# Narrowing w3 and w_out by quarters, a new order of the first loads, wider list one-hots and larger grants

## The chip, the cores and the metric

The kernel runs on one core of one Trainium2 chip. The metric is device time in microseconds: the median of 3 runs of the kernel before is 763.98 us (761.05 to 764.02). All engines of the core work at once, each in its own order: TensorE (PE; its loads of weights stand as PEld), VectorE (DVE), ScalarE (ACT), GpSimd (POOL), and SyncE (SP), which issues most transfers.

## What is computed

Three parts, each on the result of the one before:

```
attention: 4 batches, 8 heads, 576 tokens, 64 per head; heads 0-3 see the last 32 keys,
           heads 4-7 every 4th of the last 128          -> x  [2304, 512]
x2 = ((x @ w1) * (x @ w2)) @ w3 @ w_out                  w1, w2 [512, 1024], w3 [1024, 1024], w_out [1024, 512]
routing:   logits = x2 @ w_gate [512, 8]; all (token, expert) pairs in falling order of logit,
           each token taken once, each expert takes at most 288
out[t] = relu(x2[t] @ e1[e]) @ e2[e]   for the expert e of token t; e1 [8, 512, 1024], e2 [8, 1024, 512]
```

w1, w2, w3 and w_out come as 64-bit floats. The inputs are laid out for the loads beforehand; nothing else is done outside the chip.

## The kernel before

Every product runs as three products of a high and a low part (`mm(h, h)`, `mm(h, l)`, `mm(l, h)`), so each weight is split in two. A 64-bit weight is first narrowed on VectorE by three integer operations (`steps64`, lines 133, 135, 137) into a 32-bit tile `f`, of which there are two.

**Opening and batches.** Attention is a generator over 36 tiles of 64 queries (9 per batch of the input). Each `next(att)` emits half of a tile's work, software pipelined: scores of tile t (L176), its masked maximum (L190), the exponentials (L197), the normalization on GpSimd (L204), transposes of tile t-2 (L210), the product with the values for t-3 (L223), and the output split of t-4 (L243 to L246). The output of a tile stands in the single PSUM bank "rt" until L245 and L246 have read it. The queries of tile t+3 (`qk_load`, L151) and values of t+1 (`v_load`, L158) are issued by SP on the way. Before the first batch of products starts, the loop `while nxt < 4` makes 16 such halves; from the 8th on, each is followed by one narrowing step of w1 and w2.

Then `moe(b)` runs for the 4 batches: 32 groups of 12 products (L414 to L416), one group per yield, two groups (x @ w1, x @ w2) per 128 columns and half of the tokens. At each yield the loop emits a narrowing step, and attention halves of the next batch, at 0.6 halves per group. `narrow12()` narrows w1 and w2, 8 pieces of [128, 1024]; `narrow3()` then does w_out and w3, 12 pieces, one operation per yield, loads each piece (1024 KB) into slots 8 and 9, and stores each narrowed piece (512 KB) in a scratch tensor `kept`, from where the fourth batch fetches it. Slots 8 and 9 are wanted by the third batch, so whatever is left of `narrow3()` is emitted before it. SP executes its issues in program order; a load into a used buffer waits there for the buffer's last reader.

**Logits, x2 and routing.** In the fourth batch `gates()` multiplies w3, w_out and w_gate, and the logits are made from the products directly. `make_w()` multiplies w3 and w_out (W = w3 @ w_out), `make_x2()` then x2 = (a * b) @ W, and `experts()` runs the 8 experts. All three are one generator, the filler, which yields the nominal time of what it has emitted (680 ns for three products of 512 columns, 395 for three of 288). Beside it runs `routing()`: 7 rounds, each with a search of six steps (L733 to L749: a comparison matrix on VectorE, 18 small products on TensorE, a short chain on VectorE back to the next matrix), then counts (L753 to L790), and, spread over the next round, `make_list()` (L645 to L699) for the expert that was closed. It yields the time for which TensorE should be given other work: each yield grants the filler that number times PACE0 while x2 is made, and times PACE1 in the experts. Between two searches' products stand a HALF_NS (1050) and a STEP_NS (1700). All of routing uses the one bank "rt" too.

`make_list()` makes, for six of the 18 token columns at a time, a one-hot matrix [128, 6, 96] (L670) and multiplies it by six columns each (L675), three times per list, 8 lists. `x_gather(k + 1)` in expert k waits for list k+1, and `w_gather()` starts an expert's weights only after its list is there.

Of the kernel before, what the change touches and what calls it, by code (L numbers as in the profile page):

```python
# [9 lines left out]
F32 = mybir.dt.float32  # L10
# [22 lines left out]

START, ATT_RATE, LATE, EARLY, FIRST = 8, 0.6, 3, 7, 0.7

ONE, GATHER_F = 2, 2

BITE = 256

TAIL = slice(0, 2 * KB), slice(2 * KB, CAP)  # L40

PACE0, PACE1 = 1.0, 1.3
STEP_NS, FIRST_NS, LIST_NS, SUM_NS, CR_NS, SMALL_NS, HALF_NS, COPY_NS = 1700, 1550, 1800, 1800, 650, 1150, 1050, 900


# [40 lines left out]
def body(tc, qk_d, v_d, ke_d, ve_d, msk_d, cst_d, tri_d, w1_d, w2_d, w3_d, wo_d, wg_d, e1_d, e2_d, out):  # L86
# [23 lines left out]
    def slot(i, shape, dt, name):  # L110
        return xp.tile(shape, dt, tag=f"s{i}", name=name, bufs=1)

    def wtile(tag):

        return [wp.tile([128, 1024], F32R, tag=tag, name=tag + n, bufs=8) for n in "hl"]

    def split(w, h, l, eng=None):

        act(h, w, AF.Copy)
        n = 1024 if eng is None else BITE  # L120
        for i in range(0, 1024, n):
            (eng or dve).tensor_tensor(l[:, i:i + n], w[:, i:i + n], f32(h)[:, i:i + n], op=OP.subtract)
        return [h, l]

    def load64(src, t):
        nc.sync.dma_start(t.rearrange("p a b -> p (a b)"), src.bitcast(I32))
        return t

    def steps64(t, out):

        f = pm.tile([128, 1024], F32, tag="f", name="f", bufs=2)
        lo, hi, w = t[:, :, 0], t[:, :, 1], f.bitcast(I32)
        dve.tensor_scalar(w, hi, 0x07FFFFFF, 3, op0=OP.bitwise_and, op1=OP.logical_shift_left)
        yield
        dve.scalar_tensor_tensor(w, hi, -0x40000000, w, op0=OP.bitwise_and, op1=OP.bitwise_or)
        yield
        dve.scalar_tensor_tensor(w, lo, 29, w, op0=OP.logical_shift_right, op1=OP.bitwise_or)
        out.append(f)
        yield


# [138 lines left out]

    def narrow12():
        for j, (n, i) in enumerate(in12):
            f = []
            yield from steps64(got.pop(j), f)
            W[n, i] = [x.rearrange("p (k f) -> p k f", k=4)
                       for x in split(f.pop(), *wtile("wa" if n == 1 else "wb"), nc.gpsimd)]
            get12(j + 4)


# [3 lines left out]
    got3, narrowed, pre, placed = {}, {}, {}, [0]  # L293

    def get3(j):
        if j < 12:
            n, i = in3[j]
            got3[j] = load64((wo_d if n == "wo" else w3_d)[i], slot(8 + j % 2, [128, 1024, 2], I32, "w64"))

    def narrow3():  # L300
        get3(0)
        get3(1)
        for j in range(12):
            f = []
            yield from steps64(got3.pop(j), f)
            nc.sync.dma_start(kept[in3[j]], f.pop())
            get3(j + 2)

    def fetch(x, t):
        nc.sync.dma_start(t, kept[x])  # L310
# [136 lines left out]
    v_load(0)  # L447
    qk_load(1)
    qk_load(2)
    nc.sync.dma_start(C, cst_d)  # L450
    get12(0)
    nc.sync.dma_start(msk[:, 2:], msk_d[:, 2:])
    nc.sync.dma_start(wg, wg_d)
    narrow = itertools.chain(narrow12(), narrow3())
    nxt, i = 0, 0
    while nxt < 4:
        nxt = next(att)
        i += 1
        if i in (3, 6, 9):
            get12(i // 3)  # L460
        if i >= START:
            next(narrow, None)

    for b in range(B):
        if b == 3:
            stacks.pop("pa").close()
            p2 = pool("p2")
            p3 = pool("p3")
            for i in range(2):
                x = p2.tile([128, 2, 1024], F32, tag=f"P{i}", name="wo", bufs=1)  # L470
                for n in range(2):
                    fetch(("wo", 2 * i + n), x[:, n])
            fetch_w3(4)
            making_wg = gates()
        if b == 2:
            for _ in narrow:
                pass
        steps = 0
        for done, (half, f, n) in enumerate(moe(b)):
            if b == 0:  # L480
                while (n, f // 2) not in W:
                    next(narrow, None)
            if b < 2:
                next(narrow, None)
            while b < 3 and nxt is not None and nxt < NB * (b + 2) and (
                    steps < done * ATT_RATE + (min(done, 8) * FIRST if b == 0 else 0) or half == 1 and nxt < NB * (b + 1)):
                nxt = next(att, None)
                steps += 1
            if b == 3:
                if done >= LATE:  # L490
                    next(making_wg, None)
                while half == 1 and placed[0] // 2 < f // 2:
                    place3()
        while nxt is not None and nxt < NB * (b + 1) + (4 if b < 2 else 9):
            nxt = next(att, None)
# [84 lines left out]


    lists, widx, wreg = {}, {}, {}
    oh = [pm.tile([128, CAP], F32R, tag="gl", name="oh", bufs=3) for _ in range(ONE)]
    dg = pm.tile([128, CAP], F32, tag="gh", name="dg", bufs=3)
    li0 = cst.tile([KB, 3], I32, name="li0", bufs=1)

    def routing():
# [50 lines left out]
        ch = rt([128, NC, 3], "ch")  # L638
        rh = rt([128, NC, 3, 2], "rh", BF)
        pc = cc(C_PC, 108).rearrange("p (c t x) -> p c t x", c=NC, t=3)  # L640
        c3 = rt([128, 3], "c3")
        for i in range(3):
            dve.memset(c3[:, i:i + 1], float(i))

        def make_list(k):  # L645
# [20 lines left out]
            dve.tensor_tensor(rh, ch[:, :, :, None].to_broadcast([128, NC, 3, 2]), pc, op=OP.mult)  # L666
            lf = rt([KB, 6], "lf")
            for c in range(0, NC, 6):
                OH = p4.tile([128, 6, KB], BF, name="OH", tag="OH", bufs=2)
                dve.tensor_tensor(OH, rb[:, c:c + 6, None].to_broadcast([128, 6, KB]),  # L670
                                  i96[:, None, :].to_broadcast([128, 6, KB]), op=OP.is_equal)
                yield
                o = bank([KB, 6], "rt")
                for i in range(6):
                    mm(o, OH[:, i, :], rh[:, c + i].rearrange("p t x -> p (t x)"), start=(i == 0), stop=(i == 5))  # L675
                if c:
                    dve.tensor_tensor(lf, lf, o, op=OP.add)
                else:
                    dve.tensor_copy(lf, o)
            if k == 0:  # L680

                for i in range(ONE):
# [122 lines left out]
    c = 0  # L805
# [90 lines left out]
    def experts():  # L896
# [32 lines left out]
        def hid(k, f):  # L929
            xh, xl = X2[k]  # L930
            wh, wl = EW[k, 1, f // 2]
            fs = slice((f % 2) * 128, (f % 2) * 128 + 128)
            a = bank([128, CAP], "h")
            for d in range(4):
                mm(a, wh[:, d, fs], xh[:, d, :], start=(d == 0), stop=False)  # L935
                mm(a, wh[:, d, fs], xl[:, d, :], start=False, stop=False)  # L936
                mm(a, wl[:, d, fs], xh[:, d, :], start=False, stop=(d == 3))  # L937
                yield 395
            h, l = [pm.tile([128, CAP], F32R, tag="g" + s, name="h" + s, bufs=3) for s in "hl"]
            HH[k, f] = h, l  # L940
            act(h, a, AF.Relu)  # L941
            dve.scalar_tensor_tensor(l, a, 0.0, f32(h), op0=OP.max, op1=OP.subtract)  # L942
# [158 lines left out]
```

## Time and profile before

| | |
|---|---|
| median of 3 runs | 763.98 us (761.05 to 764.02) |
| the profiled execution | 764.13 us, span 762.3 us |
| TensorE busy | 727.9 us, 95% of the span |
| VectorE, ScalarE, GpSimd busy | 54%, 46%, 39% |
| mean granted clock of TensorE | 0.984 |

The span goes from the first to the last instruction; the time of the execution includes what lies around it. TensorE's products overlap, so their times are not to be added up: what one of them occupies is read from the distance of two starts. "Idle" in a row is followed by what ended it. Stages by TensorE's lines: opening to 30.4 us, the four batches from there, from 112, from 182 and from 249, the logits from 317, make_w from 329, x2 from 381 to 503, experts from 509 to 755.

### The profile page before, as it was taken

How to read it: one execution, taken by the hardware profiler on the slowest of the kernel's cores; microseconds unless marked ns; L12 is line 12 of the kernel's file. 1: busy time of each engine (PE TensorE's matmuls, PEld its weight loads, DVE VectorE, ACT ScalarE, POOL GpSimd, SP SyncE). 2: the span in 40 equal slices, each digit the busy share in tenths (PEclk: the TensorE clock that was granted, in tenths of full speed). 3: DMA queues.
4: the chain of work that ended last, by engine and by line, in shares of the span. 5: the costliest groups of instructions: out<-in, count | busy, mean ns of one | idle time of the engine just before them, and what ended most of it. 6: DMA issues, size and time to landing. Idle time of an engine off the chain costs nothing.

```text
span 762.3 us, 17301 instructions
## 1 busy us (share of the span) xinstructions
PE 727.9 (95%) x6708; PEld 660.5 (87%) x6708; DVE 411.5 (54%) x1363; ACT 354.4 (46%) x832; POOL 298.3 (39%) x356
## 2 busy tenths in 40 slices
PE   5699999899999999999999999899999999999996
PEld 3589899899999888877877777689999999999996
DVE  4977778832321101147786767778787752233401
ACT  5665534444442213321455466335666656655511
POOL 1866211101100004715264265435466475665411
PEclk9699999999999999999999999999999999999998
DMA  9984899732200503111699799868797799996111
GB/s 317 322 248 131 300 331 315 271 107 66 73 28 1 221 4 109 34 42 44 111 110 133 118 133 205 192 204 212 222 257 221 190 257 264 252 284 211 46 32 33
DMA packets 57411, 126.76 MB, mean 166 GB/s; under 512 B 9584, under 2 KB 27120, under 8 KB 54768
## 3 DMA queue, kind: packets, MB, share of 16 engines
q1 hardware_dynamic: 27088, 89.46, 35.1%
q0 software_dynamic: 27648, 31.46, 24.0%
q10 hardware_dynamic: 2592, 4.72, 1.7%
q8 instruction: 53, 0.87, 0.5%
q14 instruction: 30, 0.25, 0.1%
HBM read 87.87 MB, written 15.73 MB: 136 GB/s over the span
## 4 chain that ended last, share of the span: by engine, by line
PE 76%; DVE 9%; issue 7%; ACT 3%; POOL 2%; DMA 2%; SPq 1%; POOLq 0%; DVEq 0%; ACTq 0%
PE ps_ab L414 10%; PE ps_ab L415 9%; PE ps_ab L416 9%; PE ps_ab L554 4%; PE ps_ab L555 3%; PE ps_ab L556 3%; PE ps_h L935 3%; PE ps_h L937 3%; PE ps_h L936 3%; PE ps_ab L956 3%; PE ps_ab L958 3%; PE ps_ab L957 3%; PE ps_rt L223 3%; PE ps_rt L744 2%; PE ps_ab L523 2%
## 5 line engine op out<-in xcount | busy, mean ns | idle before, releaser
L420 DVE TENSOR_TENSOR g<-a,ps_ab 128x256 f32<-128x256 f32 (+1 forms) x64 | 28.9, 452 | 137.3 <-PE ps_ab L416 130.0
L204 POOL TENSOR_TENSOR p<-p,sm 128x384 f32<-128x384 f32 x36 | 37.7, 1047 | 154.6 <-ACT p L197 77.4
L414 PE MATMUL ps_ab<-x,wbh 128*128 128x256 f32 (+1 forms) x256 | 78.8, 308 | 0.0
L414 PE MATMUL ps_ab<-x,wah 128*128 128x256 f32 (+1 forms) x256 | 78.7, 307 | 0.0
L956 PE MATMUL ps_ab<-hh,w 128*128 128x288 f32 (+1 forms) x256 | 77.4, 302 | 0.0
L439 POOL DMA_DIRECT2D wbl<-g x40 | 52.2, 1705 | 63.2 <-ACT wbl L437 53.2
L416 PE MATMUL ps_ab<-x,wal 128*128 128x256 f32 (+1 forms) x256 | 76.2, 298 | 0.0
L415 PE MATMUL ps_ab<-x,wah 128*128 128x256 f32 (+1 forms) x256 | 76.2, 298 | 0.0
L416 PE MATMUL ps_ab<-x,wbl 128*128 128x256 f32 (+1 forms) x256 | 76.0, 297 | 0.0
L415 PE MATMUL ps_ab<-x,wbh 128*128 128x256 f32 (+1 forms) x256 | 75.9, 297 | 0.0
L958 PE MATMUL ps_ab<-hh,w 128*128 128x288 f32 (+1 forms) x256 | 74.7, 292 | 0.0
L957 PE MATMUL ps_ab<-hl,w 128*128 128x288 f32 (+1 forms) x256 | 74.6, 291 | 0.0
L942 DVE SCALAR_TENSOR_TENSOR hl<-ps_h,hh 128x288 fp32r<-128x288 f32 x64 | 29.1, 455 | 78.9 <-ACT hh L941 78.9
L419 ACT ACTIVATE a<-ps_ab 128x256 f32<-128x256 f32 (+1 forms) x64 | 26.1, 408 | 97.5 <-PE ps_ab L416 97.5
L941 ACT ACTIVATE hh<-ps_h 128x288 fp32r<-128x288 f32 x64 | 26.4, 412 | 95.2 <-PE ps_h L937 95.2
L197 ACT ACTIVATE p<-p,sm 128x96 f32<-128x96 f32 x144 | 52.1, 363 | 38.6 <-DVE sm L190 38.6
L554 PE MATMUL ps_ab<-Wx,wbh 128*128 128x512 f32 x144 | 60.2, 418 | 0.0
L555 PE MATMUL ps_ab<-Wx,wbh 128*128 128x512 f32 x144 | 56.8, 394 | 0.0
L556 PE MATMUL ps_ab<-Wx,wbl 128*128 128x512 f32 x144 | 56.8, 394 | 0.0
L414 PEld LDWEIGHTS ps_ab<-x,wbh 128*128 128x128 f32 x256 | 48.6, 190 | 3.1 <-issue 1.0
L414 PEld LDWEIGHTS ps_ab<-x,wah 128*128 128x128 f32 x256 | 48.9, 191 | 2.6 <-issue 1.0
L416 PEld LDWEIGHTS ps_ab<-x,wal 128*128 128x128 f32 x256 | 49.0, 192 | 0.0
(269 smaller groups left out, 2160.6 us busy)
## 6 DMA issues: line engine op xcount, KB each, us to landing
w<-w_dram SPq DMA_DIRECT2D x16, 1024.0 KB, 8.5
est<-e_dram SPq DMA_DIRECT2D x31, 512.0 KB, 5.3
qk<-qk_dram SPq DMA_DIRECT2D x36, 320.0 KB, 5.0
yt<-e_dram SPq DMA_DIRECT2D x22, 512.0 KB, 5.6
wbl<-g POOLq DMA_DIRECT2D x32, 256.0 KB, 5.7
v<-v_dram SPq DMA_DIRECT2D x36, 192.0 KB, 4.0
kept<-f SPq DMA_DIRECT2D x12, 512.0 KB, 4.1
w<-est POOLq DMA_DIRECT2D x12, 512.0 KB, 6.7
```

The lines of the kernel that those rows point to most:

```text
L197: act(p[:, i, :], p[:, i, :], AF.Exp, bias=sm[:, 1, i:i + 1], scale=-1.0, accum_out=sm[:, 2, i:i + 1])
L204: nc.gpsimd.tensor_tensor(p, p, sm[:, 3, :, None].to_broadcast([128, 4, KB]), op=OP.mult)
L414: mm(a, wh[:, k, fs], xh[:, k, ts], start=(k == 0), stop=False)
L415: mm(a, wh[:, k, fs], xl[:, k, ts], start=False, stop=False)
L416: mm(a, wl[:, k, fs], xh[:, k, ts], start=False, stop=(k == 3))
L439: nc.gpsimd.dma_start(x, src, accum_op=OP.add)
L554: mm(a, h[:, f, :], wh, start=(f == 0), stop=False)
L555: mm(a, h[:, f, :], wl, start=False, stop=False)
L556: mm(a, l[:, f, :], wh, start=False, stop=(f == 7))
L956: mm(y, wh[:, f % 2, ds_], h[:, ns], start=(f == 0 and (not b or d == 0)), stop=False)
L957: mm(y, wh[:, f % 2, ds_], l[:, ns], start=False, stop=False)
L958: mm(y, wl[:, f % 2, ds_], h[:, ns], start=False, stop=(f == 7 and (not b or d == 3)))
```

## The change

Four things change together. (1) The table C is split: its first 128 columns (the identity, 64 KB) are loaded where it was, the rest and wg after the opening loop. The first load of w1 moves from before the loop to its 3rd half, the next ones from the 3rd, 6th, 9th to the 6th, 9th and 12th, and a mask part to the 13th. (2) w_out and w3 are loaded and narrowed in 48 quarters of 256 columns, the three operations of a quarter at once, at 0.62 quarters per product group once w1 and w2 are done, through the third batch; they have three buffers of their own in place of slots 8 and 9. Tiles "gl" and "gh" move from the pool `pm` to `p4`, which opens later. (3) The one-hot matrix has 32 more columns, zero and never written again, and each product takes 128 columns of it as weights, the first 96 being its own. (4) PACE0 goes from 1.0 to 1.15, PACE1 from 1.3 to 1.4.

```diff
+LATER = 0.62
-PACE0, PACE1 = 1.0, 1.3
+PACE0, PACE1 = 1.15, 1.4
...
-    def steps64(t, out):
+    def steps64(t, f):
-        f = pm.tile([128, 1024], F32, tag="f", name="f", bufs=2)
...
     def get3(j):
-        if j < 12:
-            n, i = in3[j]
-            got3[j] = load64((wo_d if n == "wo" else w3_d)[i], slot(8 + j % 2, [128, 1024, 2], I32, "w64"))
+        if j < 48:
+            n, i = in3[j // 4]
+            t = got3[j] = pa.tile([128, 256, 2], I32, tag="w3q", name="w64", bufs=3)
+            nc.sync.dma_start(t.rearrange("p a b -> p (a b)"),
+                              (wo_d if n == "wo" else w3_d)[i][:, 256 * (j % 4):256 * (j % 4) + 256].bitcast(I32))
 
     def narrow3():
         get3(0)
         get3(1)
-        for j in range(12):
-            f = []
-            yield from steps64(got3.pop(j), f)
-            nc.sync.dma_start(kept[in3[j]], f.pop())
+        for j in range(48):
+            if j % 4 == 0:
+                f = pm.tile([128, 1024], F32, tag="f", name="f", bufs=2)
+            for _ in steps64(got3.pop(j), f[:, 256 * (j % 4):256 * (j % 4) + 256]):
+                pass
+            yield
             get3(j + 2)
+            if j % 4 == 3:
+                nc.sync.dma_start(kept[in3[j // 4]], f)
...
-    nc.sync.dma_start(C, cst_d)
-    get12(0)
-    nc.sync.dma_start(msk[:, 2:], msk_d[:, 2:])
-    nc.sync.dma_start(wg, wg_d)
-    narrow = itertools.chain(narrow12(), narrow3())
+    nc.sync.dma_start(ident, cst_d[:, C_ID:C_ID + 128])
+    narrow, later = narrow12(), narrow3()
     nxt, i = 0, 0
     while nxt < 4:
         nxt = next(att)
         i += 1
-        if i in (3, 6, 9):
-            get12(i // 3)
+        if i in (3, 6, 9, 12):
+            get12(i // 3 - 1)
+        if i == 13:
+            nc.sync.dma_start(msk[:, 2:], msk_d[:, 2:])
         if i >= START:
             next(narrow, None)
 
+    nc.sync.dma_start(C[:, C_STK:], cst_d[:, C_STK:])
+    nc.sync.dma_start(wg, wg_d)
+    owed = 0.0
     for b in range(B):
         if b == 3:
+            for _ in later:
+                pass
...
-        if b == 2:
-            for _ in narrow:
-                pass
...
-            if b < 2:
-                next(narrow, None)
+            if b < 3:
+                if len(W) < 8:
+                    next(narrow, None)
+                else:
+                    owed += LATER
+                    while owed >= 1:
+                        owed -= 1
+                        next(later, None)
...
+        OHs = [rt([128, 6 * KB + 32], f"OH{i}", BF) for i in range(2)]
+        for x in OHs:
+            dve.memset(x[:, 6 * KB:], 0.0)
...
-                OH = p4.tile([128, 6, KB], BF, name="OH", tag="OH", bufs=2)
-                dve.tensor_tensor(OH, rb[:, c:c + 6, None].to_broadcast([128, 6, KB]),
+                OHs.reverse()
+                OH = OHs[0]
+                dve.tensor_tensor(OH[:, :6 * KB].rearrange("p (c j) -> p c j", c=6), rb[:, c:c + 6, None].to_broadcast([128, 6, KB]),
...
-                o = bank([KB, 6], "rt")
+                o = bank([128, 6], "rt")
                 for i in range(6):
-                    mm(o, OH[:, i, :], rh[:, c + i].rearrange("p t x -> p (t x)"), start=(i == 0), stop=(i == 5))
+                    mm(o, OH[:, KB * i:KB * i + 128], rh[:, c + i].rearrange("p t x -> p (t x)"), start=(i == 0), stop=(i == 5))
```

## Rows read from the trace of the kernel before

**Rows 1.** The page, part 1: busy us (share of the span) and instructions per engine.
```profile
PE 727.9 (95%) x6708; PEld 660.5 (87%) x6708; DVE 411.5 (54%) x1363; ACT 354.4 (46%) x832; POOL 298.3 (39%) x356
```

**Rows 2.** Stretches: length, busy us (instructions) by engine, granted clock, DMA share, GB/s.
```profile
0.00:30.40 30.40, 16.41 (x212) 11.71 (x212) 19.12 (x83) 18.19 (x72) 11.35 (x15) 0.84 0.96 321
...
112.00:182.00 70.00, 67.40 (x726) 63.85 (x725) 43.04 (x155) 29.82 (x122) 9.87 (x10) 1.00 0.59 204
182.00:248.80 66.80, 66.80 (x702) 63.42 (x702) 17.79 (x96) 24.99 (x96) 5.79 (x7) 1.00 0.13 39
...
381.00:503.40 122.40, 117.66 (x894) 93.54 (x891) 90.07 (x315) 60.84 (x87) 61.43 (x55) 0.99 0.91 154
...
508.80:624.00 115.20, 112.59 (x1071) 110.20 (x1072) 88.05 (x276) 70.24 (x110) 67.77 (x85) 1.00 0.83 223
```

**Rows 3.** TensorE's waits, whole span: us in total, times, longest.
```profile
PE ps_ab L176 <- DMA qk<-qk_dram: 7.8, 4, 3.8
PE ps_rt L744 <- DVE r_Gt L733: 4.7, 5, 2.1
```

**Rows 4.** Timeline of the opening: start us, us, engine, line, operation; idle before.
```profile
3.58 0.43 SPq L126 DMA_DIRECT2D w<-w_dram  x1
...
9.48 1.09 PE L210 MATMUL ps_h<-C,p 128*96 128x128 f32 x4 [0.91 <-POOL p L204]
...
12.65 1.03 PE L176 MATMUL ps_ab<-qk 64*64 64x96 f32 x16 [2.08 <-DMA qk<-qk_dram]
...
14.72 0.66 DVE L133 TENSOR_SCALAR f<-w 128x1024 int32<-128x1024 int32 x1
...
17.06 0.33 SPq L126 DMA_DIRECT2D w<-w_dram  x1
...
34.07 1.30 DVE L133 TENSOR_SCALAR f<-w 128x1024 int32<-128x1024 int32 x1 [0.62 <-POOL wbl L122]
```

**Rows 5.** Transfers issued in 3:4, then 16.9:19.9: count, KB each, us to landing.
```profile
w<-w_dram SPq DMA_DIRECT2D x1, 1024.0 KB, 7.3
...
w<-w_dram SPq DMA_DIRECT2D x1, 1024.0 KB, 11.2
```

**Rows 6.** Timeline, 133 to 139.5 us.
```profile
135.49 0.69 DVE L133 TENSOR_SCALAR f<-w 128x1024 int32<-128x1024 int32 x1 [2.50 <-DMA w<-w_dram]
...
138.03 0.69 PE L223 MATMUL ps_rt<-pt,v 96*64 96x64 f32 x16 [2.60 <-issue]
```

**Rows 7.** VectorE's groups, 60 to 160 us: busy, mean ns of one, idle before.
```profile
L133 DVE TENSOR_SCALAR f<-w 128x1024 int32<-128x1024 int32 x14 | 10.3, 734 | 9.9 <-DMA w<-w_dram 5.9 <-DMA w<-wo_dram 4.0
```

**Rows 8.** Transfers issued, 156 to 240 us.
```profile
qk<-qk_dram SPq DMA_DIRECT2D x6, 320.0 KB, 3.2
```

**Rows 9.** TensorE's timeline, 493 to 498 us.
```profile
493.04 0.62 PE L744 MATMUL ps_rt<-r_Gt,r_CR 128*128 128x40 bf16 x18
493.51 0.48 PE L554 MATMUL ps_ab<-Wx,wbh 128*128 128x512 f32 x1
...
494.97 0.39 PE L675 MATMUL ps_rt<-r_rh,OH 128*96 128x6 bf16 x6
495.22 0.47 PE L554 MATMUL ps_ab<-Wx,wbh 128*128 128x512 f32 x1
```

**Rows 10.** Weight loads of L675, then L744: ns min/median/max, first and last start.
```profile
L675 PEld LDWEIGHTS <-OH x144: 119/125/202, 378.6 to 623.3; 128*96 128x96 bf16 x144
...
L744 PEld LDWEIGHTS <-r_CR x756: 95/96/102, 339.3 to 588.5; 128*128 128x128 bf16 x189
```

**Rows 11.** Timeline, 474 to 490 us.
```profile
479.05 3.90 POOL L122 TENSOR_TENSOR wal<-est,wah 128x256 fp32r<-128x256 f32 x4
...
479.06 3.26 DVE L662 SCALAR_TENSOR_TENSOR r_rb<-r_rk 128x18 bf16<-128x18 f32 x1
...
484.17 0.61 PE L744 MATMUL ps_rt<-r_Gt,r_CR 128*128 128x40 bf16 x18 [2.11 <-DVE r_Gt L733]
```

**Rows 12.** Stretch with TensorE's granted clock, columns as in rows 2.
```profile
484.00:488.00 4.00, 3.83 (x32) 3.09 (x32) 3.26 (x12) 0.31 (x1) 0.00 (x0) 0.64 0.90 298
```

More of the change, by code (lines that the diff above doesn't have):

```diff
@@ L137, in steps64 @@
         dve.scalar_tensor_tensor(w, lo, 29, w, op0=OP.logical_shift_right, op1=OP.bitwise_or)
-        out.append(f)
         yield
@@ L282, in narrow12 @@
         for j, (n, i) in enumerate(in12):
-            f = []
+            f = pm.tile([128, 1024], F32, tag="f", name="f", bufs=2)
             yield from steps64(got.pop(j), f)
             W[n, i] = [x.rearrange("p (k f) -> p k f", k=4)
-                       for x in split(f.pop(), *wtile("wa" if n == 1 else "wb"), nc.gpsimd)]
+                       for x in split(f, *wtile("wa" if n == 1 else "wb"), nc.gpsimd)]
             get12(j + 4)
@@ L302, in narrow3 @@
         get3(1)
-        for j in range(12):
-            f = []
-            yield from steps64(got3.pop(j), f)
-            nc.sync.dma_start(kept[in3[j]], f.pop())
+        for j in range(48):
+            if j % 4 == 0:
+                f = pm.tile([128, 1024], F32, tag="f", name="f", bufs=2)
+            for _ in steps64(got3.pop(j), f[:, 256 * (j % 4):256 * (j % 4) + 256]):
+                pass
+            yield
             get3(j + 2)
+            if j % 4 == 3:
+                nc.sync.dma_start(kept[in3[j // 4]], f)
     def fetch(x, t):
@@ L582, in body @@
     lists, widx, wreg = {}, {}, {}
-    oh = [pm.tile([128, CAP], F32R, tag="gl", name="oh", bufs=3) for _ in range(ONE)]
-    dg = pm.tile([128, CAP], F32, tag="gh", name="dg", bufs=3)
+    oh = [p4.tile([128, CAP], F32R, tag="gl", name="oh", bufs=3) for _ in range(ONE)]
+    dg = p4.tile([128, CAP], F32, tag="gh", name="dg", bufs=3)
     li0 = cst.tile([KB, 3], I32, name="li0", bufs=1)
@@ L668, in make_list @@
             for c in range(0, NC, 6):
-                OH = p4.tile([128, 6, KB], BF, name="OH", tag="OH", bufs=2)
-                dve.tensor_tensor(OH, rb[:, c:c + 6, None].to_broadcast([128, 6, KB]),
+                OHs.reverse()
+                OH = OHs[0]
+                dve.tensor_tensor(OH[:, :6 * KB].rearrange("p (c j) -> p c j", c=6), rb[:, c:c + 6, None].to_broadcast([128, 6, KB]),
                                   i96[:, None, :].to_broadcast([128, 6, KB]), op=OP.is_equal)
                 yield
-                o = bank([KB, 6], "rt")
+                o = bank([128, 6], "rt")
                 for i in range(6):
-                    mm(o, OH[:, i, :], rh[:, c + i].rearrange("p t x -> p (t x)"), start=(i == 0), stop=(i == 5))
+                    mm(o, OH[:, KB * i:KB * i + 128], rh[:, c + i].rearrange("p t x -> p (t x)"), start=(i == 0), stop=(i == 5))
                 if c:
-                    dve.tensor_tensor(lf, lf, o, op=OP.add)
+                    dve.tensor_tensor(lf, lf, o[:KB], op=OP.add)
                 else:
-                    dve.tensor_copy(lf, o)
+                    dve.tensor_copy(lf, o[:KB])
             if k == 0:
@@ L938, in hid @@
                 yield 395
-            h, l = [pm.tile([128, CAP], F32R, tag="g" + s, name="h" + s, bufs=3) for s in "hl"]
+            h, l = [p4.tile([128, CAP], F32R, tag="g" + s, name="h" + s, bufs=3) for s in "hl"]
             HH[k, f] = h, l
```

## The prediction

> **What bounds the kernel now.** I read the page first, then the stretches by stage, then TensorE's waits, then the timeline where those waits are. On the page TensorE is busy for 95% of the span and no other engine for more than 54%, setting aside the weight loads that run beside it [rows 1]. So only three things shorten the kernel: TensorE idling less, TensorE at a low granted clock for less time, or TensorE having less to do. By stage [rows 2], the opening (0 to 30.4 us) holds 30.4 − 16.41 = 14.0 us of idle time at a mean granted clock of 0.84. The second batch takes 70.0 us with 2.6 us idle. The third, with the same tiles and products, takes 66.8 us with no idle time at all. While x2 is made beside routing (381 to 503.4) 4.7 us are idle, and in the experts beside routing (508.8 to 624) 2.6 us. The waits with names are the queries' loads (7.8 us, of which 3.8 is the very first load) and routing's comparison matrix (4.7 us in five waits) [rows 3]. All sums below are against the profiled execution: 764.13 us, of which 762.3 is the span. It is 0.15 us above the median of 763.98, so I carry no correction.
>
> **Opening.** TensorE's tile 3 starts at 12.65 after waiting for its queries [rows 4]. Ahead of them SP has issued the table C (310 KB), the first weight (1024 KB), a mask (48 KB) and wg (16 KB). The change leaves 64 KB of C there; 246 + 1024 + 48 + 16 = 1334 KB move behind, 1.37 MB, which is 4.3 us at the 321 GB/s of this stretch [rows 2]. The queries then come near 8.3, but tile 0's transposes stand before tile 3 in TensorE's order, start at 9.48 on GpSimd's result and take 1.09 us. So tile 3 starts near 10.6, 2.1 us sooner, and VectorE, which begins narrowing right behind that tile, would begin at 14.72 − 2.1 = 12.6 [rows 4].
>
> The price is on SP's queue: each weight is now issued one position later. The first one is issued at 3.58 and lands 7.3 us later, at 10.9 [rows 4, 5]. It gets two query loads and one value load in front (832 KB) and loses 246 KB: 0.60 MB net, 1.9 us, landing at 12.8. The next two move less against their use. The fourth (issued at 17.06, landing 11.2 us later at 28.3) is now also behind the fifth weight, a query, a value and a ke load: 1632 − 310 = 1322 KB, 1.35 MB, 4.2 us, so 32.5. Its first narrowing runs at 34.07 now [rows 4] and would be wanted at 34.07 − 1.9 = 32.2. That leaves about 1.6 us of gain; I take **−1.5 us**. The rest of C, the mask and wg go out after the first tiles in a stretch where the transfers are full anyway; their users come later, so they cost nothing unless the ring is late again. Bounds: −4.2 if every tile followed its load, +2.5 if the fourth weight is late by as much as the longest wait for a weight [rows 6].
>
> **w3 and w_out by quarters over three batches.** Before, 36 operations of 1024 columns are pushed into two batches behind 1 MB loads. VectorE waits 9.9 us for loads there [rows 7]. One of these waits shows how it reaches TensorE [rows 6]: VectorE sits 2.50 us until the load lands at 135.49, does its narrowing, and only then reaches L245, which frees the one bank "rt"; TensorE's L223 wants that bank and stands 2.60 us. After, there are 48 loads of 256 KB, each followed by three operations of 256 columns in one go, at 0.62 steps per product group (12 products; 32 groups in a batch). w1 and w2 are done after 16 groups of the first batch, so (16 + 32 + 32) × 0.62 = 49.6 steps cover the 48 and the closing store, and nothing is left to drain before the fourth batch. VectorE gets 108 more operations; at 734 ns per 1024 columns for the first kind [rows 7] a quarter costs between 184 and 734 ns, and the third batch has 66.8 − 17.79 = 49 us of VectorE free [rows 2], so they are hidden. SP issues 36 more loads and 12 stores at the same places as now; none waits for the store of its own block, because the load is issued before it.
>
> Is a quarter early enough? It is asked for one step before its use: 1 / 0.62 = 1.6 groups of 66.8 / 32 = 2.1 us, 3.4 us. A 320 KB load takes 3.2 us in the third batch [rows 8], and SP runs ahead of VectorE, so most loads are in time, and the block is shorter than before. I take the second batch to become like the third but for a rest: **−2.5 us**. Bounds: −3.2 (70.0 to 66.8, all of it), and +3.2 (the third batch becomes like the second and the second stays).
>
> **List one-hots 128 wide.** 24 groups of six products use 96 columns of a weight tile. From the starts on TensorE [rows 9], six of them occupy 495.22 − 494.97 = 0.25 us (42 ns each), and 18 of routing's, with all 128 columns, 493.51 − 493.04 = 0.47 us (26 ns each). A load of weights takes 125 ns with 96 columns and 96 ns with 128 [rows 10]. At 26 ns, 144 products save 144 × 16 = **−2.3 us**, all in stretches where TensorE is the bound. Bounds: 0 and −2.3. The zeroed 32 columns cost two small memsets once.
>
> The rows here go against a rule in the Trainium skill, TensorE: Matmul & The Clock Gate, "LDWEIGHTS (loading the stationary operand)": the load takes its columns divided by 1.2 ns, so 128 columns take 27 ns longer than 96, and the change would cost 144 × 27 ns, an estimated 3.8 us, where the forecast has a gain. This case's trace disagrees: 96 ns against 125 ns, the wide one being the faster.
>
> **Grant.** Between two of the search's products the filler is given 1050 + 1700 = 2750 ns; 1.15 makes it 412 ns more, 1.4 in place of 1.3 275 ns more. VectorE must fit its chain into that. The five waits for L733 sum to 4.7 us, the longest 2.1 [rows 3]; 412 ns off each is 2.1 us, and the smaller stalls lose a part too. The longest is followed by a granted clock of 0.64 over 4 us, 4 × 0.36 = 1.4 us, partly at the 1.2 GHz level [rows 12]; half of that may go. Against it, about 0.65 of a routing round moves into the experts and takes its own small stalls along. I take **−3 us**. Bounds: −8.7 (4.7 + 2.6 idle in both stretches [rows 2] and the clock's 1.4) and +2 (one new stall like the longest).
>
> Longer routing must not starve the experts. A round is 29.5 us by the yields in the code, and make_w, make_x2 and first_in offer 146 us of filler, so 146 / (29.5 × 1.15) = 4.3 rounds instead of 5 are done when the experts begin. The other 2.7 rounds at 1.4 take 111 us, the last lists 25 us more; an expert is 28 us of filler. List 5, the tightest, is ready at 98 us of it and its rows are gathered at 121; list 6 at 123 against 149. So no expert waits. The cover is 23 us; if it were gone, TensorE would stand for the difference.
>
> Sum: −1.5 − 2.5 − 2.3 − 3 = −9.3, 764.1 − 9.3 = 754.8, so **755 us**.
>
> **Rivals.** (1) The grant buys nothing. The longest stall began with L662, 18 elements wide, taking 3.26 us from 479.06, while GpSimd started a subtraction group of 3.90 us at 479.05; TensorE then waited 2.11 us at 484.17 [rows 11]. Stalls that start like this depend on where the collision falls, and 412 ns hardly touches them. The other terms stand: 764.1 − 6.3 = 757.8. Against it: the same steps leave a smaller delay if the filler is longer. The Trainium skill, SBUF — State Buffer, "SBUF: two separate sides", states that VectorE and GpSimd share a pair of ports by an exclusive lock and the loser blocks for the whole instruction. That is this rival's mechanism, and it would leave the stalls as they are; the trace agrees in this one place.
>
> (2) The opening loses: a weight comes late, or TensorE stays at the low clock longer. +3 instead of −1.5: 759.3. For it: four weights with margins of a few tenths by my working; against: tile 3 is surely earlier.
>
> (3) The wide one-hots gain nothing, since their six windows overlap at steps of 96 columns as no load of before does: 757.1.
>
> (4) Slower: the quarters come too late. Each is issued only one step ahead, 3.4 us against 3.2 us of landing in a quiet stretch [rows 8]. If query loads and 512 KB stores make that 4.5 us, VectorE stands about 1 us before a step. Where a step comes right before L245 (0.62 of 22 tiles, 14), TensorE pays as in [rows 6]: 14 us. Then 764.1 − 6.8 + 14 = 771. It decides from 0.75 us per such tile (10.6 / 14), where the total passes +0.5%. Against it: of 9.9 us of such waits only this one of 2.5 us shows as a TensorE wait of its own.
>
> (5) The low clock of the opening gets shorter: 30.4 us at 0.84 lack 4.9 us [rows 2]; if those go as well, 754.8 − 4.9 = 750.
>
> **Numbers.** Forecast 0.50 (its own range 751 to 758), (1) 0.20, (2) 0.12, (3) 0.05, (4) 0.07, (5) 0.06. About 0.5%, 3.8 us, is what a measurement here can tell from no change. Faster by more: nearly all of the forecast (0.49), 0.17 of (1), 0.07 of (2), 0.04 of (3), all of (5): 0.83. Slower: most of (4), 0.06. Within: 0.11. The range of 747 to 763 reaches from below (5) past (2) and leaves (4) out.
>
> **What would show it.** Right: tile 3 at about 10.6 and narrowing from about 12.8; no TensorE wait over 1 us at L223 in the second batch, and that batch under 68 us; L675's six products in 0.16 us; waits for L733 under 3 us in all; the last list near 655. Wrong: narrowing waits of a microsecond before L245 in the third batch; the fourth weight landing after 34; the same sum of waits for L733; an expert waiting for a list.

## The result and the profile after

The changed kernel takes 767.81 us (median of 20 runs) against 763.89 for the kernel before beside it: a ratio of 1.0060 with a 95% interval of 1.0044 to 1.0075. It is slower, where 755 was forecast. The profiled execution took 766.63 us with a span of 764.8, so it lies 1.2 us below the median; the one before lies 0.2 us above its own. In all that follows, a kernel's difference is taken from its ratio to the kernel before on the same chip; stage lengths are distances between the starts of stages on TensorE in the profiles, and the hand-over is the time from the start of x2's last three products to that of the experts' first.

The page after, part 1, as in [rows 1]:

```profile
PE 728.2 (95%) x6708; PEld 660.6 (86%) x6708; DVE 431.5 (56%) x1473; ACT 355.2 (46%) x832; POOL 296.7 (39%) x356
```

The sum of busy time says nothing: TensorE has 728.2 us against 727.9. The stages say it (columns as in [rows 2]): opening, second batch, third batch, x2, the hand-over from x2 to the experts, and the experts beside routing.

```profile
0.00:29.60 29.60, 16.25 (x213) 11.71 (x213) 19.23 (x83) 18.17 (x72) 11.10 (x15) 0.79 0.95 323
110.40:180.30 69.90, 67.60 (x726) 63.97 (x725) 46.24 (x196) 30.03 (x120) 7.44 (x9) 1.00 0.60 188
180.30:251.80 71.50, 68.74 (x702) 65.13 (x701) 40.02 (x153) 25.36 (x97) 6.62 (x8) 0.98 0.43 139
...
381.40:493.70 112.30, 111.24 (x808) 88.10 (x804) 76.42 (x275) 60.69 (x87) 56.81 (x49) 1.00 0.96 153
493.70:509.60 15.90, 10.89 (x62) 9.57 (x60) 7.58 (x19) 2.86 (x7) 7.80 (x13) 0.68 0.81 256
509.60:624.00 114.40, 113.47 (x1142) 110.61 (x1143) 88.07 (x267) 70.01 (x108) 63.99 (x82) 1.00 0.80 216
```

The opening is 0.8 us shorter. The second batch has not changed (69.9 against 70.0), and the third has become like it: 71.5 against 66.8, with 2.8 us idle where there was none. x2 is ten microseconds shorter, as more of routing now runs in the experts. But the hand-over takes 16.4 us, against 6.1 before; the 15.9 us of it shown here have 5 us idle and a mean granted clock of 0.68.

TensorE's waits after, as in [rows 3] (us in total, times, longest):

```profile
PE ps_ab L176 <- DMA qk<-qk_dram: 6.4, 2, 3.7
PE ps_rt L223 <- issue: 5.2, 3, 2.6
PE ps_h L904 <- DMA rows<-x_d,li: 4.5, 3, 2.6
...
PE ps_rt L763 <- DVE r_Gt L752: 1.1, 1, 1.1
```

The comparison matrix (L744 before, L763 now) has gone from 4.7 us to 1.1, and the queries from 7.8 to 6.4. Two waits have grown: at L223, for the bank "rt", and a new one, for the first expert's rows gathered from the scratch copy of x2.

**The wait at L223.** VectorE's waits for loads over the first 260 us are about as long in total as before, 10.8 us against 9.9 [rows 7]:

```profile
DVE f L134 <- DMA w<-wo_dram: 5.6, 4, 2.0
DVE f L134 <- DMA w<-w_dram: 5.2, 6, 2.1
```

What has changed is where they stand: before, the last one ended at 147.33, in the second batch; now two are in the third. The timeline at the third batch (start, us, engine, line; idle before in brackets) has one like that in [rows 6]:

```profile
189.69 0.43 SPq L151 DMA_DIRECT2D qk<-qk_dram  x1
190.23 0.37 SPq L300 DMA_DIRECT2D w<-w_dram  x1
190.65 0.42 SPq L315 DMA_DIRECT2D kept<-f  x1
...
195.50 0.29 DVE L134 TENSOR_SCALAR f<-w 128x256 int32<-128x256 int32 x1 [2.14 <-DMA w<-w_dram]
...
196.63 0.28 DVE L245 TENSOR_TENSOR x<-ps_rt,x 128x128 fp32r<-128x128 f32 x1
...
197.31 0.69 PE L223 MATMUL ps_rt<-pt,v 96*64 96x64 f32 x16 [2.59 <-issue]
```

This is the 34th quarter of the 48, issued at 190.23 between a query load of 320 KB and a store of 512 KB. VectorE wants it at 195.50 − 2.14 = 193.36, 3.1 us later, and gets it 5.3 us after the issue. Counted so, nine of the 48 quarters are waited for, 10.5 us in all (the tenth of the waits above, 0.3 us, is for the first load of w1), and they come 3.7 to 5.3 us after their issue. L245, behind the narrowing in VectorE's order, frees the bank, and L223 starts 2.59 us late. The stretches of 2 us around it show that this is not the whole price: after the gap the clock granted falls to about half, the 1.2 GHz level, for most of 4 us.

```profile
196.00:198.00 2.00, 0.69 (x18) 0.66 (x20) 1.95 (x13) 0.60 (x3) 0.00 (x0) 1.00 0.07 26
198.00:200.00 2.00, 2.00 (x21) 1.78 (x22) 0.18 (x1) 2.00 (x10) 0.83 (x1) 0.52 0.52 137
200.00:202.00 2.00, 2.00 (x13) 2.00 (x13) 0.17 (x1) 0.14 (x1) 0.00 (x0) 0.63 0.84 294
```

2 × 0.48 + 2 × 0.37 = 1.7 us are lost there on top of the gap. With the 2.8 us idle in this batch that is 4.5 of the 4.7 us by which it grew, so nearly all of them hang on this one quarter. It is no accident of one execution: of the four kernels below that keep these quarters as they are, `u_grant`, `u_loads` and `m_tail` have the gap at L223 too, 2.3 to 2.8 us long, between 198.6 and 199.5, with the low clock behind it and a third batch of 71.2 to 71.7 us. `u_lists` has 1.66 us there, no low clock, and 69.1. Before, the gap of [rows 6] was as long, but no low clock followed it:

```profile
138.00:140.00 2.00, 1.97 (x38) 1.81 (x39) 1.97 (x12) 1.87 (x9) 0.83 (x1) 1.00 0.51 167
```

Why one such gap is followed by the low clock and another isn't, no run shows.

**The hand-over from x2 to the experts.** The rows of the first expert are gathered from x2 after it was stored. The timeline of that trip:

```profile
481.03 1.06 ACT L121 ACTIVATE wah<-est 128x1024 fp32r<-128x1024 f32 x1 [7.71 <-DMA est<-e_dram]
482.61 0.33 ACTq L564 DMA_DIRECT2D x_d<-xr  x1
485.86 1.06 ACT L873 ACTIVATE w<-est 128x1024 fp32r<-128x1024 f32 x1 [3.28 <-DMA est<-e_dram]
488.52 0.33 ACTq L564 DMA_DIRECT2D x_d<-xr  x1
491.67 1.01 POOL L888 DMA_INDIRECT rows<-x_d,li  x1 [2.47 <-DVE r_mw L728]
...
493.69 0.39 PE L571 MATMUL ps_ab<-Wx,wbl 128*128 128x512 f32 x1
494.25 0.91 POOL L888 DMA_INDIRECT rows<-x_d,li  x1 [0.30 <-issue]
...
498.66 0.74 PE L904 MATMUL ps_h<-dg,rows 96*128 96x96 f32 x2 [2.60 <-DMA rows<-x_d,li]
```

ScalarE stands for expert weights (L121, L873), and the stores of x2 at 482.61 and 488.52 stand behind these in its order. The gathers go out from 491.67 to 494.25, the last product of x2 is at 493.69, and the products that use the rows wait three times, for the longest until 498.66. Before, the gathers were no sooner, but x2 went on to 502.8, and the rows were there at its end, without a wait, as the same lines of that timeline have it:

```profile
493.54 1.01 POOL L869 DMA_INDIRECT rows<-x_d,li  x1 [2.50 <-DVE OH L670]
...
496.73 0.91 POOL L869 DMA_INDIRECT rows<-x_d,li  x1 [0.30 <-issue]
...
503.44 0.80 PE L885 MATMUL ps_h<-dg,rows 96*128 96x96 f32 x6
```

In the changed kernel the clock follows once more:

```profile
494.00:496.00 2.00, 0.49 (x3) 0.30 (x2) 1.25 (x2) 1.12 (x2) 1.72 (x3) 1.00 0.79 236
496.00:498.00 2.00, 0.06 (x1) 0.00 (x0) 1.97 (x3) 0.07 (x1) 2.00 (x3) 1.00 1.02 299
498.00:500.00 2.00, 0.93 (x3) 0.69 (x4) 1.12 (x2) 0.00 (x0) 1.08 (x6) 0.61 0.37 133
500.00:502.00 2.00, 2.00 (x10) 2.00 (x11) 0.00 (x0) 0.00 (x0) 0.79 (x1) 0.50 0.94 256
...
506.00:508.00 2.00, 2.00 (x25) 1.85 (x25) 0.64 (x4) 0.05 (x1) 0.00 (x0) 0.50 1.01 254
```

It waits for 4.5 us in three pieces, and the clock stands at the 1.2 GHz level until after 508: 2 × 0.39 + 8 × 0.50 = 4.8 us. The two are 9.3 of the 10.3 us by which the hand-over grew.

### The profile page after: what moved, and what is told of

Same layout as the page of the kernel before. It is cut to its first block, busy times and chain, and to the rows that moved or that the text cites. A ratio compares the mean times of both kernels' runs of the same rounds, so it can differ in the third digit from the quotient of the medians.

```text
span 764.8 us, 17468 instructions
## 1 busy us (share of the span) xinstructions
PE 728.2 (95%) x6708; PEld 660.6 (86%) x6708; DVE 431.5 (56%) x1473; ACT 355.2 (46%) x832; POOL 296.7 (39%) x356
## 4 chain that ended last, share of the span: by engine, by line
PE 74%; issue 8%; DMA 5%; DVE 5%; ACT 4%; POOL 3%; SPq 0%; POOLq 0%; ACTq 0%; DVEq 0%
PE ps_ab L422 9%; PE ps_ab L423 8%; PE ps_ab L424 8%; PE ps_h L954 3%; PE ps_ab L569 3%; PE ps_ab L975 3%; PE ps_h L956 3%; PE ps_h L955 3%; PE ps_ab L977 3%; PE ps_ab L570 3%; PE ps_ab L571 3%; PE ps_ab L976 3%; PE ps_rt L223 2%; PE ps_rt L763 2%; PE ps_ab L538 2%
## 5 line engine op out<-in xcount | busy, mean ns | idle before, releaser
L204 POOL TENSOR_TENSOR p<-p,sm 128x384 f32<-128x384 f32 x36 | 35.4, 983 | 161.0 <-ACT p L197 113.6
L569 PE MATMUL ps_ab<-Wx,wbh 128*128 128x512 f32 x144 | 58.9, 409 | 0.0
L570 PE MATMUL ps_ab<-Wx,wbh 128*128 128x512 f32 x144 | 56.1, 390 | 0.0
L422 PEld LDWEIGHTS ps_ab<-x,wbh 128*128 128x128 f32 x256 | 48.9, 191 | 3.2 <-issue 1.2
L423 PEld LDWEIGHTS ps_ab<-x,wbh 128*128 128x128 f32 x256 | 49.1, 192 | 0.0
```

The costliest lines, as they stand in the source:

```text
L204: nc.gpsimd.tensor_tensor(p, p, sm[:, 3, :, None].to_broadcast([128, 4, KB]), op=OP.mult)
L422: mm(a, wh[:, k, fs], xh[:, k, ts], start=(k == 0), stop=False)
L423: mm(a, wh[:, k, fs], xl[:, k, ts], start=False, stop=False)
L569: mm(a, h[:, f, :], wh, start=(f == 0), stop=False)
L570: mm(a, h[:, f, :], wl, start=False, stop=False)
```

## The experiments

Theory A: the quarters cost time because each is asked for one step ahead only, so late loads stand in front of L245 on VectorE; asked for earlier, they give the forecast 2.5 us. Its rival: 48 quarters cost time whenever they come, by VectorE's additional work or by the transfers. Theory B: the larger grants shorten x2 but TensorE then reaches the experts before their rows do; its rival: the search's stalls are only moved, and no cure of the trip of rows brings them back.

**One part undone at a time.** `u_quarters` takes back the 48 quarters, `u_grant` the grants (both lines `PACE0, PACE1 = 1.0, 1.3`), `u_lists` the 128 columns, `u_loads` the order of the first loads.

```diff
u_quarters:
-        for j in range(48):
+        for j in range(12):
...
u_grant:
-PACE0, PACE1 = 1.15, 1.4
+PACE0, PACE1 = 1.0, 1.3
u_lists:
-                    mm(o, OH[:, KB * i:KB * i + 128], rh[:, c + i].rearrange("p t x -> p (t x)"), start=(i == 0), stop=(i == 5))
+                    mm(o, OH[:, i, :], rh[:, c + i].rearrange("p t x -> p (t x)"), start=(i == 0), stop=(i == 5))
u_loads:
-    nc.sync.dma_start(ident, cst_d[:, C_ID:C_ID + 128])
+    nc.sync.dma_start(C, cst_d)
+    get12(0)
...
```

> The changed kernel with w3 and w_out loaded and narrowed as before (12 pieces of 1024 columns, two batches); the rest stays changed. Theory (the quarters' loads are asked for one step ahead and come late, so VectorE stands before L245 and TensorE behind it, now in the third batch too): the third batch falls from 71.5 to about 67 us, the second stays near 70, total near 763.5, 4 to 5 us under the changed kernel. Rival (the quarters gain 2.5 us as predicted and the 4.7 us of the third batch were one bad moment of one execution): 768 to 770.

> The changed kernel with the grants of before, 1.0 and 1.3; the rest stays changed. Theory (what the larger grant saves in make_w and x2 is given back where the experts' first rows are gathered, because TensorE arrives before them): make_w and x2 take 10 to 13 us longer, the stretch from the end of x2 to the experts goes from 16.4 back to about 6 us, total within 2 us of the changed kernel, 766 to 769. Rival 1 (the grant is a clean gain of 3 us, as predicted): 771. Rival 2 (the grant is what makes the kernel slower): 764 or less.

> The changed kernel with one-hots of 96 columns as before; the rest stays changed. If TensorE pays each of the 144 products: 2.3 us slower, 770. If part of them falls where TensorE waits for the gathered rows anyway: 768 to 769.

> The changed kernel with the first loads in the order of before (C whole, the first weight, the mask and wg ahead of the tile 3 queries); the rest stays changed. By the two profiles the new order gains 0.8 us before the first batch and 0.9 in it: 769.5. If the opening is the same either way: 767.8.

| | ratio to before (95%) | the part is worth, against 1.0060 |
|---|---|---|
| quarters undone | 0.9984 (0.9964 to 1.0004) | +0.76%, 5.8 us lost |
| grants undone | 1.0029 (1.0006 to 1.0052) | +0.31%, 2.4 us lost |
| 96 columns again | 1.0080 (1.0049 to 1.0111) | −0.20%, 1.5 us gained |
| old order of loads | 1.0070 (1.0046 to 1.0095) | −0.10%, 0.8 us gained |

(0.0076 × 763.9 = 5.8, and so on.) The four sum to +5.9 us where 4.6 were measured. The quarters are the main loss; of the others the ratios alone can't tell much, their intervals being 1.8 to 2.4 us to either side, and that of the changed kernel 1.2. The stages show more: without the quarters the third batch is 66.8 us long as before; without the grants the hand-over is 7.0 us in place of 16.4 and x2 with make_w is 11 us longer.

**`m_early`: the load is asked for right behind the step, not at the start of the next one.**

```diff
+            get3(j + 2)
             yield
-            get3(j + 2)
             if j % 4 == 3:
                 nc.sync.dma_start(kept[in3[j // 4]], f)
```

> The changed kernel with each quarter's load issued right behind the step that frees its buffer, one step (1.6 product groups, 3.4 us) sooner; same operations, same loads. Theory (loads asked for too late): VectorE's waits for w3 and w_out fall from about 9 us to under 4, the third batch falls from 71.5 to 67 or 68 and the second to 68 or 69, total 3 to 6 us under the changed kernel, 762 to 764. Rival (it is the operations on VectorE in one go, or the stores, that delay L245): batches stay at 70 and 71, total 767.

The ratio to the kernel before is 0.9945 (0.9927 to 0.9964): 8.8 us less than the changed kernel, more than the 3 to 6 expected. Second and third batch (columns as in [rows 2]), and VectorE's wait for these loads in the first 260 us:

```profile
111.00:178.40 67.40, 67.28 (x726) 63.73 (x726) 45.60 (x196) 30.01 (x120) 7.48 (x10) 1.00 0.61 196
178.40:246.20 67.80, 67.27 (x702) 63.76 (x701) 39.65 (x153) 25.35 (x97) 6.59 (x8) 1.00 0.46 142
```

```profile
DVE f L134 <- DMA w<-w_dram: 0.8, 2, 0.6
```

The same bytes, the same 48 × 3 operations, issue and first use now lie 4.7 to 11 us apart, and one quarter is waited for, for 0.2 us, in place of nine for 10.5 (the rest of the 0.8 us is again the first load of w1); the batches are 67.4 and 67.8. The store stays behind the `yield`, so a quarter no longer goes out together with it, but that isn't what helps: the 48 loads land 2.9 to 6.9 us after their issue here, 3.9 in the median, no sooner than the late ones before. What has changed is that they are asked for earlier. So A holds, and its rival falls. Against the kernel with the quarters undone the quarters now gain 0.9984 − 0.9945 = 0.39%, 3.0 us, with about 2 us to either side, near the 2.5 forecast for them. With three buffers a quarter could be asked for one step sooner still; that was not tried.

**`m_tail` and `q_tail`: a smaller grant at the end of x2.** If x2 is too fast only for its rows, routing could be given less filler there. From the chunk in which the gathers are asked for to the experts, 0.6 stands in place of 1.15; `q_tail` does that with the quarters undone.

```diff
+            if c == NC - ONE:
+                phase[0] = 2
...
-        want += ns * (PACE0, PACE1)[phase[0]]
+        want += ns * (PACE0, PACE1, 0.6)[phase[0]]
```

> The changed kernel with the grant lowered from 1.15 to 0.6 per ns of routing from the 17th of x2's 18 chunks until the experts begin (then 1.4 as changed). Theory (TensorE runs the last chunks in one go, arrives before the rows that went through DRAM, idles 5 us and then works at half clock): with routing's products spread between the last chunks, the wait for the gathered rows goes to under 1 us, the stretch from the end of x2 to the experts falls from 16.4 to 10 us or less, x2 grows by 3 to 6, the clock stays at 1.00 there, total 3 to 6 us under the changed kernel, 762 to 764. Rival (the gather is late whatever TensorE does, since the stores ahead of it wait for the experts' weights on ScalarE): the wait only moves, total 766 to 769.

> Both causes taken away: w3 and w_out narrowed as before, the grant 1.15, lowered to 0.6 for the last two chunks of x2 until the experts begin, 1.4 in the experts; first loads and one-hots as changed. If the two causes are separate and the rest gains as found: the narrowing gives 5 us, the lower grant at the end 3 to 5: 757 to 760, faster than the kernel before by 3 to 6 us. If the hand-over's loss only moves: 762.

Ratios: 1.0067 (1.0041 to 1.0093) and 1.0023 (1.0000 to 1.0047). The first is no better than the changed kernel's 1.0060, the second 3.0 us slower than the 0.9984 with the quarters undone; both were expected to gain. TensorE's waits in `m_tail`:

```profile
PE ps_rt L765 <- DVE r_rk L678: 5.9, 3, 4.2
```

The wait for rows is gone from the list, and the hand-over is down to 10.5 us, but TensorE now stands as long for routing's own chain, 4.2 us of it within x2, up to 496.48, with the clock at 0.50 from 498 to 500, and x2 is 8.0 us longer. The loss was moved, as the rival forecast. The rival's reason doesn't show: the rows were there in time, as soon as TensorE came later.

**`b_grant`: the kernel before with the larger grants alone.**

```diff
-PACE0, PACE1 = 1.0, 1.3
+PACE0, PACE1 = 1.15, 1.4
```

> The kernel before with the grants 1.15 and 1.4 and nothing else. Theory (saved in make_w and x2, given back at the hand-over to the experts): make_w and x2 together 10 to 12 us shorter, the stretch from the end of x2 to the experts about 16 us, TensorE waiting about 5 us for gathered rows, total 0 to 2 us above the kernel before. Rival (the larger grant is a gain of 3 us by itself and something else in the change spoils it): 3 us under the kernel before.

1.0016 (0.9991 to 1.0041): no gain. x2 with make_w is 162.2 us, against 173.5 before, the hand-over is 15.7, against 6.1, with this wait, and from the experts' first product to TensorE's last it is 2.9 us more than before (250.7 against 247.8):

```profile
PE ps_h L885 <- DMA rows<-x_d,li: 4.0, 2, 2.2
```

So it is the grant by itself, not its meeting with the other parts: of the 11.3 us taken from make_w and x2, 9.6 come back at the hand-over and 2.9 behind it, where the routing that is left over runs.

**The trip of the rows made shorter.** `m_order` is `m_early` with the splits of expert weights emitted behind the store of a chunk of x2 in place of ahead of it; `m_xr2` is `m_order` with a buffer of its own for the last chunk that the gathers need, so that its copy doesn't wait for the store before. `m_early_g` and `m_xr2_g` are `m_early` and `m_xr2` with the grants of before.

```diff
m_order, against m_early:
-            if c >= 11:
-                w_split()
-            if c >= 10:
-                w_gather()
...
+                if f == 3:
+                    if c >= 11:
+                        w_split()
+                    if c >= 10:
+                        w_gather()
m_xr2, against m_order:
+            if c == NC - ONE - 1:
+                r = slot(9, [128, 2048], F32, "r")[:, :D]
m_early_g against m_early, m_xr2_g against m_xr2:
-PACE0, PACE1 = 1.15, 1.4
+PACE0, PACE1 = 1.0, 1.3
```

> The changed kernel with quarters asked for one step sooner (as in the run before of that kind), and w_split and w_gather emitted in each chunk of x2 behind the store of the chunk before it instead of ahead of it. Theory (the rows are late because on ScalarE the copies that split the experts' weights wait for their loads, 7.7 and 3.3 us, ahead of the last stores to DRAM): the last store before the gather goes out 3 to 4 us sooner, the wait for the gathered rows falls from 6.1 to under 2.5 us, less of the first products run at half clock, total 4 to 6 us under the 760.7 of the earlier quarters alone, 755 to 757. Rival (the trip of store and gather itself is what is late): the wait stays at 5 to 6 us and the total at 760 to 761.

> The quarters asked for one step sooner, and the grants of before, 1.0 and 1.3; one-hots and first loads as changed. If the grants cost what undoing them gave back with the late quarters, 1 to 2 us: 759. If the grants were only dear through the late quarters: 761 or more.

> As the kernel with earlier quarters and the experts' weight copies behind the stores, and the chunk whose store the first gather waits for gets a buffer of its own, so that its copy on ScalarE no longer waits 4.2 us for the store of the chunk before it to land. Theory (the trip from that chunk's product to the gathered rows took about 16 us, and TensorE had 10.9 us of products for it): the store goes out about 3 us sooner, the wait for the rows falls from 3.3 to under 1 us; where TensorE then no longer stands long enough for its clock to fall, the stretch from the end of x2 to the experts goes from 15.6 to 10 us or less and the total from 758.7 to 753. If the clock falls all the same: 757.

> The same with the grants of before, 1.0 and 1.3. If the larger grant is worth something once the trip of the rows is covered: 2 to 4 us slower than with 1.15 and 1.4, 756 to 758. If it is worth nothing even then: the same time or less.

| | ratio to before (95%) | median us | x2 | hand-over |
|---|---|---|---|---|
| m_early, 1.15 and 1.4 | 0.9945 (0.9927 to 0.9964) | 760.69 | 111.1 | 17.9 |
| m_early_g, 1.0 and 1.3 | 0.9939 (0.9917 to 0.9960) | 758.77 | 121.0 | 6.7 |
| m_order, 1.15 and 1.4 | 0.9932 (0.9907 to 0.9956) | 758.72 | 110.8 | 15.6 |
| m_xr2, 1.15 and 1.4 | 0.9921 (0.9894 to 0.9949) | 757.01 | 110.8 | 14.7 |
| m_xr2_g, 1.0 and 1.3 | 0.9883 (0.9853 to 0.9913) | 754.08 | 115.6 | 7.3 |

The ratios are what to compare; the medians were not all taken on one chip. With the larger grants the hand-over goes from 17.9 to 14.7 us as the gathers go out sooner (the first 0.8 us before x2's last three products in `m_early`, 2.6 before them in `m_xr2`), but TensorE is there sooner still, and the wait for rows (6.1 us in `m_early`, 3.3 in `m_order`, 2.9 in `m_xr2`) is still followed by the low clock; the last two were expected to be under 2.5 and under 1. What is left isn't ScalarE's order: in `m_xr2` the store that the first gather needs goes out at 477.70, 9.4 us before x2's last products, against 3.9 in `m_early`, but that gather follows it 6.8 us later in place of 3.2. Why the trip got longer was not tried. In `m_xr2`:

```profile
490.00:492.00 2.00, 0.45 (x3) 0.45 (x4) 1.90 (x3) 0.63 (x2) 1.96 (x7) 1.00 1.01 229
492.00:494.00 2.00, 2.00 (x16) 1.86 (x15) 1.70 (x6) 0.00 (x0) 0.00 (x0) 0.72 0.87 231
494.00:496.00 2.00, 2.00 (x11) 2.00 (x11) 0.70 (x4) 0.00 (x0) 0.71 (x1) 0.50 0.52 82
```

In `m_xr2_g`, whose longest idle piece in the same place is 0.8 us, it doesn't fall:

```profile
492.00:494.00 2.00, 1.55 (x9) 1.17 (x7) 1.93 (x3) 0.60 (x1) 2.00 (x4) 1.00 0.84 187
494.00:496.00 2.00, 1.58 (x13) 1.41 (x13) 1.93 (x6) 0.24 (x1) 0.57 (x5) 1.00 0.87 172
```

`m_xr2_g` is faster than both kernels, by 1.2% than the one before. Its x2 is 5.4 us shorter than that of `m_early_g` at the same grants: the wait for the comparison matrix from make_w to the hand-over, 5.7 us in three in `m_early_g`, has dropped to 0.2. In `m_early_g` each of the three has a small operation of VectorE, 2.3 to 3.2 us long, beside GpSimd's subtraction for an expert's weights, as in [rows 11]. One of them:

```profile
475.13 3.88 POOL L124 TENSOR_TENSOR wal<-est,wah 128x256 fp32r<-128x256 f32 x4
475.76 2.63 DVE L768 SCALAR_TENSOR_TENSOR r_u<-r_any,r_u 128x18 f32<-128x18 f32 x1
479.84 0.33 PE L763 MATMUL ps_rt<-r_Gt,r_CR 128*128 128x40 bf16 x7 [2.06 <-DVE r_Gt L752]
```

In `m_xr2_g` that work falls at other points of the search. That was not aimed at, and as two edits lie between these kernels, which of them did it isn't shown. Whether another place of these splits would free the larger grants too was not tried; between `m_xr2` and `m_xr2_g` the ends of the intervals overlap, but no run of the one is as short as any of the other (755.92 to 760.05 us against 753.07 to 755.71, on one chip), so that the larger grants cost 2.9 us there is very likely. That they gain anything shows in no pair. So B holds as to why they don't, and of its rival this much: no cure that was tried makes them pay.

## Why the prediction was wrong

**Quarters: the step from a lead of 3.4 us and a landing of 3.2 us to "most loads are in time", and from there to a gain.** This is the term that failed most: −2.5 forecast, +5.8 measured. The lead was sized about right (2.8 to 4.2 us for the late ones). The landing was not: 3.2 us is a query load in a quiet stretch, and a quarter goes out in one bunch with query loads and the 512 KB stores, so the nine late ones took 3.7 to 5.3 us. Most were in time, 39 of 48, as the step says, but before it had been nine waits too, and now some of them stand in the third batch, where there had been none. I had this as rival (4), down to the 4.5 us of landing and the place in front of L245, with a chance of 0.07, and as the upper bound of the term (+3.2, "the third batch becomes like the second and the second stays"), which is what the stages did (+4.6 in all). Its price of 14 us on TensorE was too high: VectorE waited 10.5 us, but three waits at L223, 5.2 us in all, show for it, where before it was one of 2.6; the low clock behind the longest adds 1.7. What goes from 4.6 to the 5.8 measured lies within the intervals. `m_early` shows that the lead decided it, one line's place.

**Grants: the step "one new stall like the longest" as the upper bound, and the cover that I worked out for the lists alone.** −3 forecast, +2.4 measured by undoing (+1.2, with an interval across zero, alone). The part of it that was about the search came true: L763 waits 1.1 us in place of 4.7, and x2 has no other stall. I asked whether the lists would be ready for the experts, and they were (no list is waited for; the last one-hot products are at 659.9, 655 forecast). I did not ask it of the rows of x2. The rows before had the answer: the last gather, issued at 496.73, landed 4.5 us later, at 501.2, and the first use of the rows was at 503.44, 2.2 us on. There were two or three microseconds to spare, and x2 lost ten, while the gathers came only 2 sooner. Against `u_grant`, 11.0 us were taken from make_w and x2; 9.3 came back at the hand-over, as waits and low clock, and 2.3 behind it. Rival (1) had the result, no gain, but not by its mechanism: the collision's stalls were shortened, and lost at the hand-over. Its mechanism, stalls that depend on where GpSimd's work falls, shows elsewhere: in the 5.7 us of `m_early_g`, and in their going in `m_xr2_g`.

**Lists: right.** Six products now occupy 0.16 us, as forecast, and a weight load takes 96 ns where [rows 10] have 125:

```profile
L694 PEld LDWEIGHTS <-r_OH x144: 95/96/102, 386.8 to 660.0; 128*128 128x128 bf16 x144
...
513.86 0.30 PE L694 MATMUL ps_rt<-r_rh,r_OH 128*128 128x6 bf16 x6
514.02 0.38 PE L975 MATMUL ps_ab<-hh,w 128*128 128x288 f32 x1
```

24 × (0.25 − 0.16) = 2.2 us by the starts; undoing it cost 1.5 us, with an interval that holds both 2.3 and zero. Rival (3) falls by the starts; the ratio alone would leave it open. The Trainium skill has this case, in TensorE: Matmul & The Clock Gate, "Weight-path perf modes — Fast Weight Load (FWL) and DoubleRow": loads of exactly 128 weights of a type other than 32-bit floats take a faster way, about twice as fast. The trace agrees in kind: 125 / 96 = 1.30 ns per column against 96 / 128 = 0.75.

**Opening: right in sign, smaller in size.** Forecast −1.5; 0.8 by the stages and by the undoing. The ratio's interval for that holds zero, the stages settle it: the opening is 29.3 to 29.9 us long in all eleven kernels with the new order, and 30.2 to 30.8 in the three with the old one.

```profile
10.35 1.09 PE L210 MATMUL ps_h<-C,p 128*96 128x128 f32 x4 [1.06 <-POOL p L204]
11.37 0.92 PE L176 MATMUL ps_ab<-qk 64*64 64x96 f32 x16
...
13.81 1.23 DVE L134 TENSOR_SCALAR f<-w 128x1024 int32<-128x1024 int32 x1 [0.29 <-DMA w<-w_dram]
...
33.23 1.30 DVE L134 TENSOR_SCALAR f<-w 128x1024 int32<-128x1024 int32 x1 [0.62 <-POOL wbl L124]
```

Tile 3 starts at 11.37 (10.6 forecast), since tile 0's transposes before it came at 10.35 and not at 9.48; narrowing starts at 13.81 (12.8), and the fourth weight is in time at 33.23. Rivals (2) and (5) fall: the opening is no longer, and its granted clock is 0.79, lower than before.

The range of 747 to 763 missed the time: it left rival (4) out, and it had no case for the hand-over, because the grants were bounded by rows of the stretch that they shorten and not of the one that follows.

## What to carry to other kernels

A load asked for one step ahead needs that step to be longer than the landing in the bunch of transfers that it goes out with, not than the landing of one in a quiet stretch; where a late one would stand in front of an instruction that frees TensorE's bank, ask for it at the end of the step before, or sooner if its buffer is free. Before a stage is made shorter, look up what its successor's first operands go through (copy, store, gather) and when they arrive; beyond the slack there, a shorter stage gains nothing. Price a gap on TensorE with the low clock that may follow it.

## What was not expected of the hardware

Gaps of a few microseconds can cost more through the granted clock than I had allowed: after the one of 2.59 us before L223, at 197.31, it was 0.52 and 0.63 in the next two stretches of 2 us, and after the idle time of the hand-over 0.61 and then 0.50 until 508, 4.8 us on top of the 4.5 us of waiting. Not each gap does: after the 2.60 us of [rows 6], and after the 2.06 us before 479.84 in `m_early_g`, it stayed at 1.00. The Trainium skill describes the same in TensorE: Matmul & The Clock Gate, "HAM oscillation — how this bites in real kernels": a wait for a transfer between groups of products lets the clock fall, and the next group starts slow. These traces agree where the clock fell, and so does `m_xr2_g`, where idle pieces of under a microsecond at the same place left it at 1.00; the gap of [rows 6], behind a late transfer too, had no such fall.
